# A cubic on VectorE written as two fused operations, with the ScalarE square carrying the leading coefficient

## The chip, the cores and the metric

The kernel runs on one core of a Trainium2 chip. The metric is the device time of one execution in microseconds (us), the median of several runs. The profile names the engines PE (TensorE, with PEld for its weight loads), DVE (VectorE), ACT (ScalarE), POOL (GpSimd) and SP (SyncE, which here only issues transfers).

## What is computed

Four batches of eight heads go through a linear attention with a decaying state, and the 3072 rows of 512 that come out go through two feed-forward layers of 512 to 2048 to 512. The second layer is the one that the change touches:

```python
def _moe_ref(x, w_in, w_out):
    h = x @ w_in
    g = np.maximum(0.01 * h, h)
    return (g @ w_out).astype(np.float32)

def _moe2_ref(x, w_in, w_out):
    h = x @ w_in
    g = h - np.tanh(h)
    return (g @ w_out).astype(np.float32)
```

The elementwise function h - tanh h loses its digits where h is small, so the kernel computes it in two ways, a polynomial for small arguments and the plain difference for the others, and picks one by a mask.

## The kernel before

The program is one fixed order of instructions for each engine, written out at build time. A Python planner walks over the work in ticks. One tick is one unit of six matmuls on PE, and after each unit the planner gives ACT and DVE a credit of 1.05 times 1.29 us (`UNIT_US`) and lets queued work go out against it, so the order on ACT, DVE, SP and POOL follows from the costs that are written beside each item. At run time every engine goes through its own list in order and waits on semaphores.

All matrix products are split in high and low parts, three products for one, with one 128x512 tile as the common size. For each such tile of an operand, ACT writes the high part (`upper`, L174, tile gh) and DVE the low part by a subtraction (`lower`, L180, tile gl).

The stages are the attention, the first layer's input product (`product`, L768), the first layer's output product (the first form in `mm_half`, L693), the second layer's input product (`prod`, L1040, accumulators Xd, Yd, Zd) and its output product (the second form in `mm_half`, L693). The last two stages of each layer overlap: from about 460 us on, units of `prod` and half steps of `mm_half` alternate, with conversions of later weights (`Convert`, tiles cv and raw, stored to w2s) as background work that takes what DVE credit is left.

What a half step of the output product needs comes by a pipeline with fixed leads. Step o issues the load of tile gr for step o+4 (`load_g`, on SP, L663), the upper part for step o+3 (ACT) and the lower part for step o+2 (DVE). Weight tiles wf of `prod` are loaded four products ahead (`load_f`, SP, L886).

Around the change stands `queue_el`, which takes one 128x512 tile h of the second layer's hidden values. It runs 96 times: 24 times with `on_dve` true (the tile comes from `copy_h`), 72 times with it false (the tile comes from `join`). ACT makes u = h^2 (L969), th = tanh of h or of -h (L973), and s, a square of u plus a constant (L977). DVE then makes the small-argument value in place in s by three operations (L985, L990, L993) with a scratch tile w. For the 72 tiles the difference h - tanh h is made by an accumulating transfer on POOL's queue, which adds h onto th in SBUF (L1020, et<-h); for the other 24 DVE does it (L997). ACT then makes a mask from u (L981), DVE copies the difference over s where the mask is set (L1007), and SP stores s to DRAM (L1013, g2s), from where a later output step loads it as gr.

The 128x512 tiles come from a pool of 94 buffers, handed out first in, first out: `alloc` takes the buffer that has been free the longest, `give` puts one at the end of the list.

```python
    def alloc(nm, dt=F32, shape=(P, TB)):
        pool, tag = free.popleft()
    def give(*ts):
        for t in ts:
            _, pool, tag = home.pop(id(t))
            free.append((pool, tag))
```

`give` is called when the last user of a tile has been issued, not when it is done. Whoever gets the buffer next waits at run time until that user has finished.

Of the kernel before, what the change touches and what calls it, by code (L numbers as in the profile page):

```python
# [14 lines left out]
AF = mybir.ActivationFunctionType  # L15
# [15 lines left out]
MIN_HI = 2.0 ** -15  # L31


C3 = -0.019799353554844856
A1 = -2.6095259189605713
B1 = -0.05411865562200546
K1 = 6.448651313781738
UT = 0.125


# [34 lines left out]
def kernel(  # L75
# [12 lines left out]
    nc = tc.nc  # L88
# [23 lines left out]
    def alloc(nm, dt=F32, shape=(P, TB)):  # L112
        pool, tag = free.popleft()
        serial[0] += 1
        t = pool.tile(list(shape), dt, tag=tag, name=f"{nm}_{serial[0]}")
        home[id(t)] = (t, pool, tag)
        return t
# [845 lines left out]
    def queue_el(d, half_m, half_t, h, on_dve):  # L963
        key = 2 * (d // NG) + half_t, d % NG + NG * half_m
        e = {}

        def a1():
            e["u"] = alloc("eu")
            nc.scalar.activation(out=e["u"], in_=h, func=AF.Square)  # L969

        def a2():
            e["th"] = alloc("et")
            nc.scalar.activation(out=e["th"], in_=h, func=AF.Tanh, scale=1.0 if on_dve else -1.0)  # L973

        def a3():
            e["s"] = alloc("es")
            nc.scalar.activation(out=e["s"], in_=e["u"], func=AF.Square, bias=beta)  # L977

        def a4():
            e["mk"] = cm.tile([P, TB], BF16, tag="mk", name=f"mk_{key[0]}_{key[1]}", bufs=2)  # L980
            nc.scalar.activation(out=e["mk"], in_=e["u"], func=AF.Relu, bias=edge)  # L981

        def v1():
            e["w"] = alloc("ew")
            nc.vector.scalar_tensor_tensor(out=e["w"], in0=e["u"], scalar=C3, in1=h, op0=ALU.mult, op1=ALU.mult)  # L985

        def v2():
            if not on_dve:
                give(h)
            nc.vector.scalar_tensor_tensor(out=e["w"], in0=e["u"], scalar=A1, in1=e["w"], op0=ALU.add, op1=ALU.mult)  # L990

        def v3():
            nc.vector.scalar_tensor_tensor(out=e["s"], in0=e["s"], scalar=K1, in1=e["w"], op0=ALU.add, op1=ALU.mult)  # L993
            give(e["w"])

        def v4():
            nc.vector.tensor_tensor(out=e["th"], in0=h, in1=e["th"], op=ALU.subtract)  # L997
            give(h)

        def v5():  # L1000
            a4()
            give(e["u"])
            masks[0] += 1
            cp_q.append((tick[0] + 1, 0.76, v6))

        def v6():
            nc.vector.copy_predicated(out=e["s"], mask=e["mk"].bitcast(mybir.dt.uint16), data=e["th"])  # L1007
            masks[0] -= 1
            give(e["th"])
            defer(STORE_LAG, store)  # L1010

        def store():
            nc.sync.dma_start(out=g2s[key[0], key[1]], in_=e["s"])  # L1013
            give(e["s"])
            made2.add(key)

        def to_dve():
            t = tick[0] + 1
            if not on_dve:
                nc.gpsimd.dma_start(out=e["th"], in_=h, accum_op=ALU.add)  # L1020
            dve_q.extend([(t, 0.7, v1), (t, 0.7, v2)])
            if on_dve:
                dve_q.append((t, 0.7, v4))
            dve_q.append((t, 0.7, lambda: (v3(), mk_q.append((max(tick[0], t + (0 if on_dve else 5)), 0.72, v5)))))
            return 0.0, 0.0

        t = tick[0] + (1 if on_dve else 2)
        act_q.extend([(t, 0.62, a1), (t, 0.62, a2), (t, 0.72, lambda: (a3(), later(1, to_dve)))])
# [170 lines left out]
```

## Time and profile before

| | before |
|---|---|
| median of 3 runs | 1058.73 us (1057.42 to 1059.09) |
| the profiled execution, its own time | 1059.45 us |
| its span, first to last instruction | 1057.7 us |
| PE busy | 1041.5 us, 98% |
| DVE busy | 826.7 us, 78% |
| ACT busy | 721.1 us, 68% |
| POOL busy | 93.2 us, 9% |

The span is what the trace covers; the execution's own time has 1.75 us around it. The granted TensorE clock is at its upper level, 2.4 GHz, in every slice. An engine's busy time is the sum of its instructions. PE's records overlap, since matmuls are pipelined, so its idle time is read from the waits and from the timeline.

### The profile page before, as it was taken

The numbers are of one execution on the slowest core, as the hardware profiler recorded it, in microseconds if no ns is written. First come the engines' busy times: TensorE is split into PE (matmuls) and PEld (weight loads), VectorE is DVE, ScalarE is ACT, GpSimd is POOL, SyncE is SP. The second block draws the span as 40 slices with busy tenths as digits, with TensorE's granted clock in tenths as the row PEclk, the third lists the DMA queues.
The fourth block names the chain that finished last, engine by engine and source line by source line (L and its number), as shares of the span: only waits on it lengthen the run. The fifth ranks groups of instructions, "written<-read, shape, count | busy, mean of one in ns | idle before, by whom it ended". The sixth has DMA issues, their size and how long they took to land.

```text
span 1057.7 us, 17635 instructions
## 1 busy us (share of the span) xinstructions
PE 1041.5 (98%) x5931; PEld 902.2 (85%) x5931; DVE 826.7 (78%) x1363; ACT 721.1 (68%) x1299; POOL 93.2 (9%) x124
## 2 busy tenths in 40 slices
PE   9999899999999999999999999999999999999998
PEld 6888778888888888888888888888888888888887
DVE  3589897774788999967999789898878988687630
ACT  6889676766776556656777679887668766666440
POOL 3232000000000000000110111001100110011000
PEclk9999999999999999999999999999999999999999
DMA  9998465675668899959999988998987988878641
GB/s 223 242 269 233 164 234 190 208 250 210 225 234 286 287 361 388 393 200 285 276 323 298 324 257 260 303 290 261 316 252 224 268 246 255 259 220 229 190 149 40
DMA packets 208634, 267.67 MB, mean 253 GB/s; under 512 B 65056, under 2 KB 106144, under 8 KB 208544
## 3 DMA queue, kind: packets, MB, share of 16 engines
q1 hardware_dynamic: 197888, 247.52, 70.1%
q0 software_dynamic: 10368, 18.88, 10.3%
q8 instruction: 47, 0.77, 0.3%
q14 instruction: 43, 0.35, 0.1%
q10 hardware_dynamic: 288, 0.15, 0.1%
HBM read 161.63 MB, written 85.98 MB: 234 GB/s over the span
## 4 chain that ended last, share of the span: by engine, by line
PE 89%; DVE 4%; DMA 3%; ACT 2%; issue 1%; SPq 0%; DVEq 0%; ACTq 0%
PE o L693 46%; PE Xd L1040 11%; PE X L768 9%; PE Yd L1040 6%; PE Y L768 4%; PE Zd L1040 3%; PE y L577 2%; PE sc L550 2%; PE Z L768 2%; PE kTp L515 1%; PE y L573 1%; PE qTp L529 1%; DVE c L781 1%; PE u L596 1%; DMA gr<-g1s 1%
## 5 line engine op out<-in xcount | busy, mean ns | idle before, releaser
L693 PE MATMUL o<-gh,wo 128*128 128x512 f32 x768 | 239.5, 379 | 0.0
L693 PEld LDWEIGHTS o<-gh,wo 128*128 128x128 f32 x768 | 145.2, 189 | 20.4
L174 ACT ACTIVATE gh<-gr 128x512 fp32r<-128x512 f32 x192 | 118.3, 621 | 54.1 <-DMA gr<-g1s 26.9
L180 DVE TENSOR_TENSOR gl<-gr,gh 128x512 fp32r<-128x512 f32 x192 | 130.1, 683 | 27.9 <-ACT gh L174 22.5
L693 PE MATMUL o<-gl,wo 128*128 128x512 f32 x384 | 145.9, 380 | 2.5 <-DVE gl L180 2.5
L693 PE MATMUL o<-w2h,gh 128*128 128x512 f32 x384 | 145.5, 379 | 0.0
L693 PE MATMUL o<-w2h,gl 128*128 128x512 f32 x384 | 145.5, 379 | 0.0
L693 PE MATMUL o<-w2l,gh 128*128 128x512 f32 x384 | 145.5, 379 | 0.0
L1020 POOL DMA_DIRECT2D et<-h x72 | 62.1, 862 | 826.9 <-DVE gl L180 424.3
L1040 PE MATMUL Xd<-xch,wf 128*128 128x512 f32 x384 | 129.5, 379 | 0.0
L768 PE MATMUL X<-xch,wg 128*128 128x512 f32 x384 | 123.2, 381 | 3.7 <-DVE wg L180 2.5
L1007 DVE COPY_PREDICATED es<-mk,et 128x512 f32<-128x512 uint16 x96 | 70.9, 742 | 44.6 <-ACT mk L981 44.6
L768 PEld LDWEIGHTS X<-xch,wg 128*128 128x128 f32 x384 | 72.4, 189 | 17.0 <-DVE wg L180 3.4
L693 PEld LDWEIGHTS o<-gl,wo 128*128 128x128 f32 x384 | 72.6, 189 | 14.3 <-DVE gl L180 4.1
L969 ACT ACTIVATE eu<-h 128x512 f32<-128x512 f32 x96 | 59.9, 624 | 33.3 <-DVE h L949 31.2
L693 PEld LDWEIGHTS o<-w2l,gh 128*128 128x128 f32 x384 | 72.6, 189 | 10.3
L693 PEld LDWEIGHTS o<-w2h,gh 128*128 128x128 f32 x384 | 72.6, 189 | 10.3
L1040 PEld LDWEIGHTS Xd<-xch,wf 128*128 128x128 f32 x384 | 72.6, 189 | 10.3
L693 PEld LDWEIGHTS o<-w2h,gl 128*128 128x128 f32 x384 | 72.6, 189 | 10.3
L1040 PE MATMUL Xd<-xcl,wf 128*128 128x512 f32 x192 | 72.8, 379 | 0.0
L768 PE MATMUL X<-xcl,wg 128*128 128x512 f32 x192 | 72.8, 379 | 0.0
L985 DVE SCALAR_TENSOR_TENSOR ew<-eu,h 128x512 f32<-128x512 f32 x96 | 65.5, 683 | 8.8 <-DMA wfs<-wg 3.2
(101 smaller groups left out, 2030.3 us busy)
## 6 DMA issues: line engine op xcount, KB each, us to landing
wf<-wfs SPq DMA_DIRECT2D x168, 256.0 KB, 4.3
g1s<-c SPq DMA_DIRECT2D x96, 256.0 KB, 2.2
gr<-g1s SPq DMA_DIRECT2D x96, 256.0 KB, 5.3
g2s<-es SPq DMA_DIRECT2D x96, 256.0 KB, 3.5
gr<-g2s SPq DMA_DIRECT2D x96, 256.0 KB, 4.2
et<-h POOLq DMA_DIRECT2D x72, 256.0 KB, 5.3
raw<-in_moe_w_in_dram SPq DMA_DIRECT2D x32, 512.0 KB, 5.7
raw<-in_moe_w_out_dram SPq DMA_DIRECT2D x32, 512.0 KB, 4.4
```

Of the source, the lines that this page charges most:

```text
L174: nc.scalar.activation(out=hi, in_=src, func=AF.Copy)
L180: nc.vector.tensor_tensor(out=lo, in0=src, in1=hi.bitcast(F32), op=ALU.subtract)
L515: nc.tensor.transpose(ps[:, b, :], d["k"][:, b].rearrange("p h d -> p (h d)"), ident)
L550: nc.tensor.matmul(sc[h][:, b, :], d["kT"][r, b, :], d["qT"][r, b, tq], start=True, stop=True)
L577: nc.tensor.matmul(place(b, h), d["v"][:, b, h, :], d["A"][h][:, b, :], start=c == 0 and b % 2 == 0, stop=b % 2 == 1)
L693: nc.tensor.matmul(ACC[j], a, il(b), start=first and i == 0, stop=last and i == 2)
L768: nc.tensor.matmul(ps, w[:, c], il(x), start=first and kt == 0 and i == 0, stop=kt == 1 and i == 2, skip_group_check=True)
L969: nc.scalar.activation(out=e["u"], in_=h, func=AF.Square)
L985: nc.vector.scalar_tensor_tensor(out=e["w"], in0=e["u"], scalar=C3, in1=h, op0=ALU.mult, op1=ALU.mult)
L1007: nc.vector.copy_predicated(out=e["s"], mask=e["mk"].bitcast(mybir.dt.uint16), data=e["th"])
L1020: nc.gpsimd.dma_start(out=e["th"], in_=h, accum_op=ALU.add)
L1040: nc.tensor.matmul(ps, a, il(b), start=nm in ("P1", "P2", "P5") and kt == 0 and j == 0, stop=kt == 1 and j == 2, skip_group_check=True)
```

## The change

The polynomial is written another way. Before, three DVE operations form w = C3 u h, then w = (u + A1) w, then s = (s + K1) w, with s = (u + B1)^2. After, ACT forms s = (SQ u + B1)^2, and DVE forms s = (s + K1) th and then s = s u (times -1 where th is the tanh of -h). Tanh takes the place of h, so the coefficients are others, and the scratch tile is gone.

As th is now an input of the first DVE operation, the accumulating transfer, which writes over th, is issued right behind that operation instead of ahead of it, and h is given back at the same place. The mask is queued six ticks after the last of the two operations where it was queued five ticks after the element's start on DVE.

```diff
-C3 = -0.019799353554844856
-A1 = -2.6095259189605713
-B1 = -0.05411865562200546
-K1 = 6.448651313781738
+SQ = 0.04557729699996048
+B1 = -0.24376608898
+K1 = 0.27391141909500494
 UT = 0.125
...
         def a3():
             e["s"] = alloc("es")
-            nc.scalar.activation(out=e["s"], in_=e["u"], func=AF.Square, bias=beta)
+            nc.scalar.activation(out=e["s"], in_=e["u"], func=AF.Square, scale=SQ, bias=beta)
...
         def v1():
-            e["w"] = alloc("ew")
-            nc.vector.scalar_tensor_tensor(out=e["w"], in0=e["u"], scalar=C3, in1=h, op0=ALU.mult, op1=ALU.mult)
-
-        def v2():
+            nc.vector.scalar_tensor_tensor(out=e["s"], in0=e["s"], scalar=K1, in1=e["th"], op0=ALU.add, op1=ALU.mult)
             if not on_dve:
+                nc.gpsimd.dma_start(out=e["th"], in_=h, accum_op=ALU.add)
                 give(h)
-            nc.vector.scalar_tensor_tensor(out=e["w"], in0=e["u"], scalar=A1, in1=e["w"], op0=ALU.add, op1=ALU.mult)
 
         def v3():
-            nc.vector.scalar_tensor_tensor(out=e["s"], in0=e["s"], scalar=K1, in1=e["w"], op0=ALU.add, op1=ALU.mult)
-            give(e["w"])
+            nc.vector.scalar_tensor_tensor(out=e["s"], in0=e["s"], scalar=1.0 if on_dve else -1.0, in1=e["u"],
+                                           op0=ALU.mult, op1=ALU.mult)
...
         def to_dve():
             t = tick[0] + 1
-            if not on_dve:
-                nc.gpsimd.dma_start(out=e["th"], in_=h, accum_op=ALU.add)
-            dve_q.extend([(t, 0.7, v1), (t, 0.7, v2)])
+            dve_q.append((t, 0.7, v1))
             if on_dve:
                 dve_q.append((t, 0.7, v4))
-            dve_q.append((t, 0.7, lambda: (v3(), mk_q.append((max(tick[0], t + (0 if on_dve else 5)), 0.72, v5)))))
+            dve_q.append((t, 0.7, lambda: (v3(), mk_q.append((tick[0] + (0 if on_dve else 6), 0.72, v5)))))
             return 0.0, 0.0
```

PE's list is the same instruction for instruction, 4876 rows in both. DVE's has 1348 rows before and 1252 now. ACT, POOL and SP have the same number of rows in another order, from the first element on. Lines of the changed kernel are six lower than those of the old one at its end, and one lower in most of its middle (gl is L180 before and L179 now). In the rows below, `DMASWk` is the semaphore of the accumulating transfers on POOL's queue, which take k = 0 to 7 in turn, and `DMAHWk` that of other transfers; the number behind a tile's name is its serial number in that program.

First, DVE, where the first elements meet the output steps (about 485 to 498 us of the old trace). Before, from the conversion step to the second lower part:

```order
L217 SCALAR_TENSOR_TENSOR cv_5615<-raw_1_5529,cv_5615 128x512 [waits DMAHW6_49,DVE_49]
L985 SCALAR_TENSOR_TENSOR ew_5727<-eu_5597,h_5565 128x512 [waits DMAHW5_49]
L990 SCALAR_TENSOR_TENSOR ew_5727<-eu_5597,ew_5727 128x512 [waits DVE_49]
L180 TENSOR_TENSOR gl_5736<-gr_5602,gh_5649 128x512 [waits DMAHW6_49,DMAHW2_49]
L993 SCALAR_TENSOR_TENSOR es_5680<-es_5680,ew_5727 128x512 [waits DMAHW0_49,DVE_49,Activation_49]
L985 SCALAR_TENSOR_TENSOR ew_5752<-eu_5682,h_5595 128x512 [waits DMAHW2_49,Activation_49]
L990 SCALAR_TENSOR_TENSOR ew_5752<-eu_5682,ew_5752 128x512 [waits DVE_49]
L993 SCALAR_TENSOR_TENSOR es_5686<-es_5686,ew_5752 128x512 [waits DVE_49,Activation_49]
L985 SCALAR_TENSOR_TENSOR ew_5766<-eu_5723,h_5628 128x512 [waits PE_49,Activation_49]
L990 SCALAR_TENSOR_TENSOR ew_5766<-eu_5723,ew_5766 128x512 [waits DVE_49]
L993 SCALAR_TENSOR_TENSOR es_5738<-es_5738,ew_5766 128x512 [waits DMAHW7_49,DVE_49,Activation_49]
L180 TENSOR_TENSOR gl_5786<-gr_5641,gh_5714 128x512 [waits DMAHW1_49,PE_49]
```

Now, between the same two lower parts and the element operations ahead of them:

```order
L989 SCALAR_TENSOR_TENSOR es_5680<-es_5680,eu_5597 128x512 [waits DVE_49]
L179 TENSOR_TENSOR gl_5734<-gr_5602,gh_5649 128x512 [waits DMAHW5_49,DMAHW2_49]
L983 SCALAR_TENSOR_TENSOR es_5686<-es_5686,et_5684 128x512 [waits Activation_49]
L989 SCALAR_TENSOR_TENSOR es_5686<-es_5686,eu_5682 128x512 [waits DVE_49]
L219 SCALAR_TENSOR_TENSOR cv_5615<-raw_1_5529,cv_5615 128x512
L983 SCALAR_TENSOR_TENSOR es_5736<-es_5736,et_5723 128x512 [waits DMAHW6_49,Activation_49]
L989 SCALAR_TENSOR_TENSOR es_5736<-es_5736,eu_5721 128x512 [waits DVE_49]
L211 TENSOR_SCALAR cv_5688<-cv_5688 128x512
L213 TENSOR_SCALAR cv_5688<-cv_5688 128x512 [waits DVE_49]
L216 SCALAR_TENSOR_TENSOR cv_5688<-raw_1_5612,cv_5688 128x512 [waits DMAHW3_49,DVE_49]
L179 TENSOR_TENSOR gl_5791<-gr_5641,gh_5712 128x512 [waits DMASW1_49]
```

The second lower part has moved ahead by 12 matmuls of the program's order, conversion steps stand where element operations stood, and its buffer is now one that an accumulating transfer (the one of es_5686) reads.

Second, DVE further on (about 511 to 517 us of the old trace), between two lower parts. Before:

```order
L180 TENSOR_TENSOR gl_5940<-gr_5811,gh_5867 128x512 [waits DMAHW7_49]
L985 SCALAR_TENSOR_TENSOR ew_5944<-eu_5882,h_5856 128x512
L1007 COPY_PREDICATED es_5842<-mk_1_5942,et_5840 128x512 [waits DMASW3_49,DVE_49,Activation_49]
L990 SCALAR_TENSOR_TENSOR ew_5944<-eu_5882,ew_5944 128x512 [waits DVE_49]
L993 SCALAR_TENSOR_TENSOR es_5886<-es_5886,ew_5944 128x512 [waits DVE_49]
L985 SCALAR_TENSOR_TENSOR ew_5971<-eu_5914,h_5880 128x512 [waits PE_49]
L990 SCALAR_TENSOR_TENSOR ew_5971<-eu_5914,ew_5971 128x512 [waits DVE_49]
L993 SCALAR_TENSOR_TENSOR es_5918<-es_5918,ew_5971 128x512 [waits DVE_49]
L180 TENSOR_TENSOR gl_5993<-gr_5859,gh_5930 128x512 [waits DMAHW4_49]
```

Now:

```order
L179 TENSOR_TENSOR gl_5934<-gr_5812,gh_5862 128x512 [waits DMAHW7_49,DMAHW3_49]
L983 SCALAR_TENSOR_TENSOR es_5910<-es_5910,et_5908 128x512 [waits DMASW3_49,Activation_49]
L989 SCALAR_TENSOR_TENSOR es_5910<-es_5910,eu_5893 128x512 [waits DVE_49]
L219 SCALAR_TENSOR_TENSOR cv_5780<-raw_1_5653,cv_5780 128x512
L983 SCALAR_TENSOR_TENSOR es_5938<-es_5938,et_5936 128x512 [waits Activation_49]
L989 SCALAR_TENSOR_TENSOR es_5938<-es_5938,eu_5924 128x512 [waits DVE_49]
L211 TENSOR_SCALAR cv_5865<-cv_5865 128x512
L213 TENSOR_SCALAR cv_5865<-cv_5865 128x512 [waits DVE_49]
L216 SCALAR_TENSOR_TENSOR cv_5865<-raw_1_5777,cv_5865 128x512 [waits DMAHW6_49,DVE_49]
L179 TENSOR_TENSOR gl_5996<-gr_5854,gh_5922 128x512 [waits DMAHW5_49,DMASW4_49]
```

The first operation of es_5910 and the lower part gl_5996 now each wait for an accumulating transfer. Transfer 3 is issued behind the first operation of es_5851, which stands seven rows ahead of this piece, and transfer 4 behind that of es_5910.

Third, ACT at the same place. Before:

```order
L969 ACTIVATE eu_5882<-h_5856 128x512 [waits DMAHW2_49,DVE_49]
L973 ACTIVATE et_5884<-h_5856 128x512 [waits DMAHW3_49]
L977 ACTIVATE es_5886<-eu_5882,lead 128x512 [waits Activation_49]
L981 ACTIVATE mk_8_5899<-eu_5792,lead 128x512
L942 ACTIVATE kp_5912<-Xd_5903 128x512 [waits DMAHW0_49,PE_49]
L969 ACTIVATE eu_5914<-h_5880 128x512 [waits DVE_49]
L973 ACTIVATE et_5916<-h_5880 128x512 [waits DMASW0_49,DVE_49]
L977 ACTIVATE es_5918<-eu_5914,lead 128x512 [waits Activation_49]
L174 ACTIVATE gh_5930<-gr_5859 128x512 [waits DMAHW4_49,DVE_49]
```

Now:

```order
L968 ACTIVATE eu_5893<-h_5847 128x512
L941 ACTIVATE kp_5906<-Xd_5896 128x512 [waits DMAHW7_49,PE_49]
L972 ACTIVATE et_5908<-h_5847 128x512 [waits DVE_49]
L976 ACTIVATE es_5910<-eu_5893,lead 128x512 [waits DMAHW7_49,DMASW3_49,Activation_49]
L173 ACTIVATE gh_5922<-gr_5854 128x512 [waits DMAHW5_49,DMASW1_49]
L968 ACTIVATE eu_5924<-h_5876 128x512 [waits DMAHW1_49,DVE_49]
L972 ACTIVATE et_5936<-h_5876 128x512
L976 ACTIVATE es_5938<-eu_5924,lead 128x512 [waits Activation_49]
```

The square es_5910 gets the buffer of the tile that transfer 3 reads, and waits for that transfer; in the old program the squares there wait for ACT alone. One element earlier es_5795 waits in the same way, for transfer 2 (`DMASW2`).

## Rows read from the trace of the kernel before

**Rows 1.** The page's first part: the span, and each engine's busy time.

```profile
span 1057.7 us, 17635 instructions
PE 1041.5 (98%) x5931; PEld 902.2 (85%) x5931; DVE 826.7 (78%) x1363; ACT 721.1 (68%) x1299; POOL 93.2 (9%) x124
```

**Rows 2.** Table by stretch: length, then busy (x instructions) of each engine, PE first.

```profile
core 0: us, PE busy (x) PEld busy (x) DVE busy (x) ACT busy (x) POOL busy (x), PEclk, DMA share, GB/s
...
463.00:550.00 87.00, 84.50 (x391) 73.11 (x390) 75.70 (x127) 60.16 (x105) 8.87 (x11) 1.00 0.92 284
550.00:620.00 70.00, 70.00 (x326) 61.26 (x325) 60.93 (x96) 50.81 (x92) 9.31 (x11) 1.00 0.99 305
...
700.00:800.00 100.00, 100.00 (x465) 87.58 (x464) 83.21 (x132) 72.57 (x130) 11.30 (x14) 1.00 0.91 278
...
980.00:1057.70 77.70, 73.65 (x342) 64.15 (x340) 26.06 (x41) 24.51 (x42) 0.86 (x1) 1.00 0.37 124
```

**Rows 3.** PE's waits from 463 us to the end: total, times, longest.

```profile
PE o L693 <- DVE gl L180: 2.5, 2, 1.8
```

**Rows 4.** PE's timeline, 494 to 523 us: the two matmuls behind an idle time.

```profile
498.24 0.48 PE L693 MATMUL o<-gl,wo 128*128 128x512 f32 x1 [1.76 <-DVE gl L180]
521.35 0.48 PE L693 MATMUL o<-gl,wo 128*128 128x512 f32 x1 [0.74 <-DVE gl L180]
```

**Rows 5.** Groups by line: the three DVE operations of the polynomial.

```profile
L990 DVE SCALAR_TENSOR_TENSOR ew<-eu,ew 128x512 f32<-128x512 f32 x96 | 66.1, 688 | 2.4
L993 DVE SCALAR_TENSOR_TENSOR es<-es,ew 128x512 f32<-128x512 f32 x96 | 66.0, 687 | 4.3
```

**Rows 6.** Groups by line: ACT's square with a constant, and its tanh.

```profile
L977 ACT ACTIVATE es<-eu,lead 128x512 f32<-128x512 f32 x96 | 68.2, 710 | 3.6 <-DVE gl L180 1.4 <-DMA wfs<-wg 1.2 <-DVE es L993 0.9
L973 ACT ACTIVATE et<-h 128x512 f32<-128x512 f32 x96 | 59.3, 617 | 0.9 <-DMA g2s<-es 0.8 <-DVE ew L985 0.2
```

**Rows 7.** Accumulating transfers, start on POOL to landing: 470 to 512, whole span, 800 to 985.

```profile
DMA to landing us min/median/max: 5.4/6.2/8.8
...
DMA to landing us min/median/max: 3.2/5.3/8.8
...
DMA to landing us min/median/max: 3.2/4.8/6.3
```

**Rows 8.** The same, one transfer each: starts near 527 and near 552 us.

```profile
et<-h POOLq DMA_DIRECT2D x1, 256.0 KB, 7.2
...
et<-h POOLq DMA_DIRECT2D x1, 256.0 KB, 7.3
```

**Rows 9.** DVE's timeline, 488 to 513 us: start, length, instruction, idle time before it.

```profile
488.41 0.69 DVE L985 SCALAR_TENSOR_TENSOR ew<-eu,h 128x512 f32<-128x512 f32 x1 [3.23 <-DMA wfs<-wg]
...
489.75 0.68 DVE L180 TENSOR_TENSOR gl<-gr,gh 128x512 fp32r<-128x512 f32 x1
...
497.50 0.68 DVE L180 TENSOR_TENSOR gl<-gr,gh 128x512 fp32r<-128x512 f32 x1
498.10 0.76 DVE L220 SCALAR_TENSOR_TENSOR cv<-raw,cv 128x512 int32<-128x512 int32 x1
...
510.52 0.68 DVE L180 TENSOR_TENSOR gl<-gr,gh 128x512 fp32r<-128x512 f32 x1
511.12 0.68 DVE L985 SCALAR_TENSOR_TENSOR ew<-eu,h 128x512 f32<-128x512 f32 x1
511.72 0.73 DVE L1007 COPY_PREDICATED es<-mk,et 128x512 f32<-128x512 uint16 x1
512.35 0.67 DVE L990 SCALAR_TENSOR_TENSOR ew<-eu,ew 128x512 f32<-128x512 f32 x1
```

**Rows 10.** ACT's timeline: a copy of an upper part that waits for its load.

```profile
514.21 0.63 ACT L174 ACTIVATE gh<-gr 128x512 fp32r<-128x512 f32 x1 [4.21 <-DMA gr<-g1s]
```

**Rows 11.** SP's waits for accumulating transfers: total, times, longest.

```profile
SPq L886 <- DMA et<-h: 15.8, 7, 4.8
...
SPq L663 <- DMA et<-h: 3.4, 2, 2.7
```

**Rows 12.** The page's sixth part: loads of gr, size and median us to landing.

```profile
gr<-g1s SPq DMA_DIRECT2D x96, 256.0 KB, 5.3
...
gr<-g2s SPq DMA_DIRECT2D x96, 256.0 KB, 4.2
```

## The prediction

> **What bounds the kernel now.** I read the page's first part, then the table by stretch, then PE's waits, then PE's timeline. PE is busy for 98% of the span and no other engine for more than 78% [rows 1]. The table shows that this is no average over unlike stages: from 550 to 620 us and from 700 to 800 us PE has no idle time at all, while DVE has 9 and 17 us of it [rows 2]. The 465 matmuls of the latter 100 us give 0.215 us each, the fixed pace of this half of the program. From 463 us on, PE waits only twice, both times for a lower part from DVE, 2.5 us together [rows 3]: 1.76 us ahead of 498.24 and 0.74 us ahead of 521.35 [rows 4]. The other 4 us of the last stretch [rows 2] are the last copies and stores behind the last matmul. The change leaves PE's list as it is, and everything ahead of the first element too. So the most it can win is 2.5 us, and what it can lose is whatever new waits reach PE.
>
> **DVE's removed operations.** 96 elements lose one operation of 0.688 us [rows 5]: 66 us less on DVE, of 826.7. All of it lies beside PE's work except where DVE is late for PE, which is in the two waits. By itself it is worth between 0 and 2.5 us. The cover is PE; if a lower part were late, it would be gone.
>
> **ACT's square.** It keeps its constant from a tile (0.710 us) and gains a scale. The tanh carries a scale without such a tile and takes 0.617 us, like a plain square [rows 6], so I put the scale at nothing. The scratch tile's end frees a buffer per element, while s, th and u are held a tick longer.
>
> **The accumulating transfer.** This is the part that matters. It started as soon as th was there; now it stands behind the first DVE operation, in DVE's order. In the same breath h's buffer goes to the free list, where some dozen buffers are in line, so it is soon handed out. I counted, in the order in which the code issues things, the matmuls between such a transfer and the SP instruction that gets the buffer: before, never under 16; now, 20 of 64 times 11 to 14. For ACT the least was 26 and is now 11; for DVE's lower parts three stand at 13. Twelve matmuls are 2.6 us; a transfer takes 5.3 us in the median from its start on POOL, and 6.2 us, never under 5.4, from 470 to 512 us [rows 7]. What gets the buffer must wait, and on an in-order engine all behind it wait too. SP already did so nine times before, for up to 4.8 us [rows 11], without cost to PE.
>
> The Trainium skill, DMA: Bandwidth & Descriptors, section Anatomy of one DMA — SWDGE (gpsimd) path, fits such a transfer as 2.0 us plus its bytes at 436 GB/s, which for 256 KB is an estimate of 2.6 us. The trace disagrees: no transfer of the 72 landed in under 3.2 us [rows 7]. By that rule the waits below would vanish and the first rival would hold.
>
> **First place, PE's 1.76 us.** I follow the new DVE list with old starts. The first lower part waits for the store `DMAHW5`, which had landed when the old L985 began at 488.41 [rows 9]; operations follow each other every 0.6 us, and a conversion shift takes 0.76 [rows 9]. So the first operation of es_5686 ends at 489.7, transfer 1 starts at 489.8 and lands at 496.0, and gl_5791, which has its buffer, ends at 496.7. Before, this part began at 497.50 [rows 9], and PE wanted it at 498.24 - 1.76 = 496.5. PE waits 0.2 us instead of 1.76. With 5.4 us it doesn't wait.
>
> **Second place, some 520 us.** Three transfers now stand in a chain. Its fifth operation from 488.4 on is the first of es_5736, whose square waits only for the store `DMAHW6`, landed by 489.75, when the old lower part that waits for it began [rows 9]. It ends at 491.7, so transfer 2 starts at 491.8 and lands at 498.0. ACT's square es_5795 waits for it, ends at 498.6, and DVE goes through ten instructions, from the first operation of es_5795 to that of es_5851: 5.9 us at the pace above, to 504.6. Transfer 3 runs from 504.7 to 510.9. ACT's es_5910 waits for it: +0.7 is 511.6. Its first operation on DVE: 512.3. Transfer 4 runs from 512.4 to 518.6, and gl_5996, which has its buffer, ends at 519.3. PE wants that part 84 matmuls after the first place: 496.7 + 84 x 0.215 = 514.8. It waits 4.5 us. The three landings carry this: at 5.4 us each, the first place costs nothing and this one 2.4; at 7.3 us, as single transfers a little later took [rows 8], the two cost 8.0 together. I take the window's median: 4.7 us for both.
>
> **Behind it.** SP's load of gr_6005 waits for transfer 5, which starts right behind 4 (first operation of es_5938, about 514.6) and lands at 520.9; the load takes 5.3 us more [rows 12], so ACT copies the upper part at 526.2 and is stopped until then, as it was for 4.21 us in the old trace [rows 10]. Mask, masked copy and lower part end at 528.8; PE, having gone on at 519.3, wants it 39 matmuls on, at 527.7. That is 1.1 us; a faster load or an engine that catches up takes it to 0; I put 0.55. At the next change of output rows (matmul 2822 of the list) an ACT copy of a PSUM bank waits for a transfer issued 22 matmuls ahead, and PE needs the bank 17 matmuls after the copy: 39 matmuls, 8.4 us, against 0.7 + 6.2 + 0.6 = 7.5 us for operation, landing and copy. It fits if DVE is on time, and costs 2 us if DVE is 3 us late, which the queue above allows; I put 1.0.
>
> **The rest.** Later transfers land in 4.8 us [rows 7]; with the operation's 0.7 that makes SP 2.9 us late where it meets one 12 matmuls on. The gr load behind it lands 4.2 us after issue [rows 12], so ACT is stopped for some 3 us. Lower parts are issued a median of 29 matmuls (6.2 us) ahead of their use, 5.5 us after their own 0.7, which covers that. I put nothing. If that cover is gone because ACT is busy, it is the second rival below.
>
> **The sum.** New waits 4.7 + 0.55 + 1.0 = 6.25 us, old ones 2.5 us: +3.75. The profiled execution took 1059.45 us, of which its span is 1057.7; it would take 1063.2. It stood 0.7 us over the median 1058.73, so for the median I forecast **1062.5 us**. With the low ends (2.4 + 0 + 0 - 2.5) it is 1058.6, with the high ones (8.0 + 1.1 + 2.0 - 2.5) 1067.3.
>
> **Rivals.** *Faster:* the transfers land soon enough and DVE, with 66 us less, is ahead: both waits go and none comes, 1058.7 - 2.5 = 1056.2. It decides at the landing time: the second place's 4.5 us fall by 1.5 for each 0.5 us less over three links, so below 4.7 us it is free. Against it, none of the transfers from 470 to 512 us took under 5.4 [rows 7]; for it, the median after 800 us is 4.8. Chance 0.08. *No change:* landings at 5.4 us, the rest hidden: 1058.6, 2.1 us to either side; 0.24. For it: SP's old waits cost PE nothing. *Much slower:* the 20 waits on SP after the first stretch each get through to PE by 0.4 us, since ACT, once stopped, has its own backlog: 1062.5 + 8 = 1070.5. Against it stand the 5.5 us of cover and DVE's lighter load; 0.08. That DVE doesn't lose the operations is excluded: its list has 96 rows fewer.
>
> **How the numbers follow.** The forecast has 0.60. About 0.2% (2.1 us) is what a measurement of this kernel tells from no change. Slower is the forecast and the much slower case, 0.68; within, 0.24; faster, 0.08. The range leaves out the faster and the much slower case, 0.16, and a little of the edges: from 1057.5, just under the low ends' sum, to 1067.3, the high ends' sum.
>
> **What would show it.** PE's waits after 463 us: 6 to 7 us in place of 2.5, the largest near 519 us on a gl that waits for a transfer et<-h. ACT's waits should name et<-h ahead of es, and SP's waits for et<-h should grow from 19 us to some 60. DVE busy should be near 761 us, ACT near 721. Wrong it would be if the transfers between 485 and 520 us landed in under 5 us, if the DVE steps ahead of es_5851 ran much earlier than 504 us, or if PE's idle time came from elsewhere.

## The result and the profile after

The changed kernel took 1070.45 us in the median of 4 runs (1068.99 to 1071.47), beside 1058.49 us for the kernel before on the same chip: a ratio of 1.0111, 95% interval 1.0096 to 1.0126. It is slower, as forecast, but by 12 us and not by 4, past the upper end of the range (1067.3). The profiled execution took 1069.76 us, its span is 1067.9 us; against the old profiled execution that is 10.3 us more, of which the span has 10.2. The other 1.7 us between the medians is how the two profiled executions lie: the old one 1 us above the median of its runs, this one 0.7 below. The two slower of the four executions (1071.14 and 1071.47 us) have a mean granted clock of 0.996 and 0.997, the two faster ones 0.998.

First the page's opening part, which answers to [rows 1]:

```profile
span 1067.9 us, 17478 instructions
PE 1045.5 (98%) x5931; PEld 903.4 (85%) x5931; DVE 769.1 (72%) x1267; ACT 721.4 (68%) x1299; POOL 94.6 (9%) x124
```

DVE's load fell by 57.6 us, ACT's and POOL's stayed (0.3 and 1.4 us more). A span of ten us more with less work points to waiting. The table by stretch (columns as in [rows 2]) says where:

```profile
463.00:550.00 87.00, 81.72 (x374) 70.05 (x373) 71.54 (x119) 58.07 (x102) 8.22 (x10) 1.00 0.90 281
550.00:620.00 70.00, 70.00 (x326) 61.29 (x325) 46.25 (x73) 50.79 (x92) 10.11 (x12) 1.00 0.97 295
620.00:700.00 80.00, 76.60 (x346) 65.93 (x344) 62.65 (x99) 65.94 (x115) 7.73 (x9) 0.98 0.85 261
700.00:800.00 100.00, 98.51 (x456) 86.29 (x457) 67.86 (x106) 69.29 (x124) 12.03 (x14) 1.00 0.89 271
```

PE loses time in two places, around 500 to 520 us and around 680 to 702 us; from 550 to 620 us it has none idle. In the later of them the granted clock is under 1.00 too. PE's waits from 463 us on (total, times, longest) and its timeline, the matmuls behind an idle time, answer to [rows 3, 4]:

```profile
PE o L692 <- DVE gl L179: 7.8, 4, 2.7
PE o L692 <- ACT st L713: 2.3, 2, 2.2
```

```profile
503.33 0.48 PE L692 MATMUL o<-gl,wo 128*128 128x512 f32 x1 [2.01 <-DVE gl L179]
507.91 0.48 PE L692 MATMUL o<-gl,wo 128*128 128x512 f32 x1 [0.43 <-DVE gl L179]
519.92 0.48 PE L692 MATMUL o<-gl,wo 128*128 128x512 f32 x1 [2.68 <-DVE gl L179]
...
684.64 0.48 PE L692 MATMUL o<-w2h,gh 128*128 128x512 f32 x1 [2.16 <-ACT st L713]
...
701.49 0.48 PE L692 MATMUL o<-w2h,gl 128*128 128x512 f32 x1 [2.73 <-DVE gl L179]
```

That is 10.1 us of waits in place of 2.5: 7.6 of the 10.2 us that the span grew by. Behind the wait at 684.64 us PE also ran slower: the table of 2 us stretches shows the lower level, 0.50 (1.2 GHz), and 6 and 8 matmuls where 2 us hold 9.3.

```profile
686.00:688.00 2.00, 2.00 (x6) 1.52 (x6) 1.05 (x3) 2.00 (x5) 0.86 (x1) 0.50 0.96 297
688.00:690.00 2.00, 2.00 (x8) 1.65 (x7) 1.10 (x2) 2.00 (x5) 0.00 (x0) 0.66 1.04 378
```

In the timeline 18 matmuls start from 684.64 to 690.18 us: 17 steps in 5.54 us instead of 17 x 0.215 = 3.66, so 1.9 us are lost there. The rest of the 10.2, 0.7 us, is made of small pieces. Each wait costs PE a little more than its listed length, since the next matmul starts 0.32 us behind the first and not 0.215 (701.49 and 701.81 us). Two stops at 540 to 542 us, of which PE's waits list 0.17 us, cost 0.6 us. Against that, PE was 0.3 us ahead of the old trace at 463 us.

Set beside the same matmuls of the old trace, PE falls behind in two steps. At 463 us it is 0.3 us ahead. The matmul of 682.10 us, the last ahead of the wait at 684.64, stands at 679.01 us in the old trace, so 3.4 us were lost up to there. The last matmul of all starts at 1063.54 us instead of 1053.27, so the later place cost 7.2 us.

What do the late engines wait for? The waits for accumulating transfers from 463 us on; for SP they answer to [rows 11]:

```profile
SPq L662 <- DMA et<-h: 73.8, 13, 9.2
...
SPq L885 <- DMA et<-h: 42.0, 9, 9.0
```

```profile
ACT gh L173 <- DMA et<-h: 12.6, 6, 3.5
...
ACT kp L941 <- DMA et<-h: 5.5, 2, 3.9
```

```profile
DVE gl L179 <- DMA et<-h: 21.0, 10, 4.9
```

Before, the same views have 19.2 us for SP, 1.8 for ACT and 1.6 for DVE. The transfers themselves took no longer on the whole: from start on POOL to landing, 463 to 1000 us, minimum, median, maximum:

```profile
DMA to landing us min/median/max: 3.2/5.2/8.3
```

So the same transfers are now waited for, in three engines. They did take longer in one part of the span, 6.4 us in the median from 620 to 800 us where it was 5.1; but the program of run 5 below has 6.4 us there too, and loses nothing. The chain of waits through the later place, followed back from 701.49 us, ends on one of them: a transfer that starts at 693.12 us, holds the buffer of a lower part until 700.7 us, and PE behind it.

```profile
693.12 7.60 DMA et<-h
700.72 0.02 issue
700.74 0.70 DVE gl L179
701.44 0.04 issue
701.49 0.70 PE o L692 x2
```

The wait at 684.64 us, for ACT's copy of a PSUM bank (st), goes back to a transfer as well. ACT's upper part got the buffer of the transfer that started at 669.02 us and landed after 6.4 us, and stood 3.50 us for it; DVE stood 4.46 us behind ACT. From there on both worked without a gap until ACT came to the copy at 684.01 us:

```profile
675.44 0.63 ACT L173 ACTIVATE gh<-gr 128x512 fp32r<-128x512 f32 x1 [3.50 <-DMA et<-h]
```

```profile
676.72 0.75 DVE L1003 COPY_PREDICATED es<-mk,et 128x512 f32<-128x512 uint16 x1 [4.46 <-ACT mk L980]
```

### The profile page after: what moved, and what is told of

Its sections match the earlier page's. It is cut to its first block, busy times and chain, and to the rows that moved or that the text cites. A ratio compares the mean times of both kernels' runs of the same rounds, so it can differ in the third digit from the quotient of the medians.

```text
span 1067.9 us, 17478 instructions
## 1 busy us (share of the span) xinstructions
PE 1045.5 (98%) x5931; PEld 903.4 (85%) x5931; DVE 769.1 (72%) x1267; ACT 721.4 (68%) x1299; POOL 94.6 (9%) x124
## 4 chain that ended last, share of the span: by engine, by line
PE 85%; DVE 5%; DMA 5%; ACT 2%; issue 2%; SPq 0%; DVEq 0%; ACTq 0%; POOLq 0%
PE o L692 43%; PE Xd L1034 10%; PE X L767 9%; PE Yd L1034 5%; PE Y L767 4%; PE Zd L1034 2%; PE Z L767 2%; PE sc L549 2%; PE y L576 2%; DMA et<-h 1%; PE kTp L514 1%; PE y L572 1%; DVE c L780 1%; PE qTp L528 1%; PE u L595 1%
## 5 line engine op out<-in xcount | busy, mean ns | idle before, releaser
L179 DVE TENSOR_TENSOR gl<-gr,gh 128x512 fp32r<-128x512 f32 x192 | 130.2, 683 | 50.0 <-ACT gh L173 24.7
L983 DVE SCALAR_TENSOR_TENSOR es<-es,et 128x512 f32<-128x512 f32 x96 | 65.8, 685 | 27.9 <-ACT es L976 27.8
L1034 PEld LDWEIGHTS Xd<-xch,wf 128*128 128x128 f32 x384 | 72.6, 189 | 10.3
L976 ACT ACTIVATE es<-eu,lead 128x512 f32<-128x512 f32 x96 | 68.1, 710 | 9.5 <-issue 4.6
```

Source lines behind the costliest of these rows:

```text
L179: nc.vector.tensor_tensor(out=lo, in0=src, in1=hi.bitcast(F32), op=ALU.subtract)
L1034: nc.tensor.matmul(ps, a, il(b), start=nm in ("P1", "P2", "P5") and kt == 0 and j == 0, stop=kt == 1 and j == 2, skip_group_check=True)
```

## The experiments

Theory A was that the loss comes from buffers handed out again while a transfer still reads them. The rivals were B, that the transfer's later start and landing delays the masked copies; D, that the new order of DVE's list makes it late; and that the loss at 680 to 702 us only follows from the one at 500 to 520 us. The runs, as ratios to the kernel before on the same chip, with PE's waits behind 463 us in the profiled execution. That is one execution of each run; in runs 3 and 10 it is 2 us faster than the run's median, in run 8 it is 1.5 us slower.

| run | ratio | 95% interval | PE waits, us |
|---|---|---|---|
| the change | 1.0111 | 1.0096 to 1.0126 | 10.1 |
| 1 its order, transfers' buffers reused later | 1.0026 | 1.0013 to 1.0038 | 3.4 |
| 2 old order, transfer behind first operation | 1.0230 | 1.0214 to 1.0245 | 19.5 |
| 3 two operations, transfer early | 1.0005 | 0.9993 to 1.0017 | 1.6 |
| 4 old kernel, all reuses on SP, near | 1.0176 | 1.0139 to 1.0213 | 13.9 |
| 5 the change, all reuses later | 0.9992 | 0.9983 to 1.0000 | 0.3 |
| 6 as 5, ahead of 613 us only | 1.0060 | 1.0045 to 1.0074 | 4.8 |
| 7 as 5, behind 613 us only | 1.0055 | 1.0040 to 1.0071 | 4.8 |
| 8 old kernel, all reuses later | 0.9991 | 0.9983 to 1.0000 | 0.6 |
| 9 as 5, for SP's loads only | 1.0080 | 1.0056 to 1.0103 | 5.7 |
| 10 as 5, for ACT and DVE only | 1.0022 | 1.0011 to 1.0033 | 1.0 |
| 11 h given back four ticks later | 1.0086 | 1.0070 to 1.0102 | 8.3 |
| 12 no transfers, DVE subtracts | 0.9972 | 0.9960 to 0.9983 | 0 |

**1. Same order, other buffers.** `alloc` passes over a young buffer; nothing else changes, and every engine's list is that of the changed kernel.

```diff
-        pool, tag = free.popleft()
+        at = next((i for i, b in enumerate(free) if tick[0] - young.get(b, -99) >= 8), 0)
+        pool, tag = free[at]
+        del free[at]
...
                 nc.gpsimd.dma_start(out=e["th"], in_=h, accum_op=ALU.add)
+                young[home[id(h)][1:]] = tick[0]
                 give(h)
```

> The changed kernel, with the same instructions in the same order on every engine; only which buffer of the free list a tile gets differs: one that an accumulating transfer still reads (given back under 8 ticks ago) is passed over. SP's least reuse distance is 38 matmuls instead of 11, ACT's 29 instead of 11, DVE's 31 instead of 13. Theory A (early reuse makes in-order SP, ACT and DVE wait for the transfer): SP's waits for et<-h fall from 116 us to under 20, PE's waits after 463 us from 10 us to under 3, the clock stays at the upper level, 1056 to 1060 us. Rival B (the transfer's later start and landing itself delays the masked copies): unchanged, 1068 to 1072. Rival D (the new order, conversions ahead of lower parts, makes DVE late): unchanged, 1068 to 1072.

1062.03 us. Of the 1.11%, 0.85 are gone, with DVE's order, the late transfers and the late masks all still there: rivals B and D fall as the main cause. SP's waits for et<-h fell from 116 to 0.3 us. It missed the expected 1060 by another wait of the same kind: passing over some buffers handed ACT's tanh one that a store of a converted weight still read. ACT's timeline, then PE's:

```profile
501.52 0.63 ACT L976 ACTIVATE et<-h 128x512 f32<-128x512 f32 x1 [6.00 <-DMA w2s<-cv]
```

```profile
504.87 0.80 PE L696 MATMUL o<-gl,wo 128*128 128x512 f32 x1 [2.48 <-DVE gl L183]
```

**2. The transfer late, all else old.** The kernel before with its three operations; the first now reads th, so the transfer must stand behind it. Its small-argument values are others by that; the work is the same.

```diff
-            nc.vector.scalar_tensor_tensor(out=e["w"], in0=e["u"], scalar=C3, in1=h, op0=ALU.mult, op1=ALU.mult)
+            nc.vector.scalar_tensor_tensor(out=e["w"], in0=e["u"], scalar=C3, in1=e["th"], op0=ALU.mult, op1=ALU.mult)
+            if not on_dve:
+                nc.gpsimd.dma_start(out=e["th"], in_=h, accum_op=ALU.add)
...
-            if not on_dve:
-                nc.gpsimd.dma_start(out=e["th"], in_=h, accum_op=ALU.add)
```

> The kernel before, in its own order with its three operations; only the first operation reads th in place of h (so the small-argument values are others), and so the transfer has to be issued behind it. h is given back at the second operation, as before. SP's reuse distances fall to 11 to 15 matmuls at 16 places, ACT's to 11 to 15 at 7, and masked copies stand 13 or more behind the transfer. Theory A: waits for et<-h on SP above 60 us, on ACT and DVE above 15 us, PE waits above 8 us after 463 us, 1066 to 1078 us though DVE's order is the old one. Rival D (the new order of DVE's list is what costs): 1057 to 1061 us.

1083.94 us, above the expected range: the old order does not save it. ACT alone waited 68 us for transfers, and PE 7.0 us at once for a copy of a PSUM bank. It is worse than the change. Its masked copies stand as near as 13 matmuls behind the transfer and waited 19.5 us for it, so this run alone doesn't separate A from B; runs 1 and 5 do.

**3. Two operations, the transfer early.** The polynomial multiplies by h, with three coefficients of its own; the transfer goes out ahead of the first operation again, and the mask has its old rule back. The main line of the edit:

```diff
-            nc.vector.scalar_tensor_tensor(out=e["s"], in0=e["s"], scalar=K1, in1=e["th"], op0=ALU.add, op1=ALU.mult)
+            nc.vector.scalar_tensor_tensor(out=e["s"], in0=e["s"], scalar=K1, in1=h, op0=ALU.add, op1=ALU.mult)
```

> Two operations as in the changed kernel, but the polynomial multiplies by h instead of th (three coefficients fitted for that form), so that the transfer goes out as early as in the kernel before, ahead of the first operation, and the mask keeps its old rule. DVE loses the same 96 operations. SP's least distances are 12 to 19 at 8 places, ACT's 24, DVE's 18. Theory A: most of the loss is gone, SP's waits for et<-h 20 to 50 us, 1056 to 1062 us. Rival D (fewer DVE operations let conversions move ahead of what PE needs): 1066 to 1071 us, as the order has moved just as much.

1060.43 us, no change against the kernel before (the interval ends at 0.17%). DVE is as light as in the change (768.7 us) and conversions have moved ahead in its list as they did there, so neither costs anything that this run can tell.

**4. All reuses on SP.** The kernel before, its order kept; loads of gr and wf take the buffer of a transfer where they can.

```diff
-        pool, tag = free.popleft()
+        at = 0
+        if nm in ("gr", "wf"):
+            at = next((i for i, b in enumerate(free) if tick[0] - young.get(b, -99) <= 1), 0)
+        pool, tag = free[at]
+        del free[at]
...
             if not on_dve:
+                young[home[id(h)][1:]] = tick[0]
                 give(h)
```

> The kernel before with the same order on every engine; a load on SP gets, where it can, the buffer that a transfer reads, so that all 72 reuses fall on SP, 13 of them at 12 matmuls and 30 at 12 to 19; ACT and DVE wait for none. It isolates SP's waits from those on ACT and DVE. Theory A1 (waits on SP alone are enough): SP's waits for et<-h above 100 us, PE loses 5 to 10 us, 1063 to 1069 us. Theory A2 (SP's waits are covered by the leads of loads, and only waits on ACT and DVE, or SP's together with them, get through): below 1060 us.

1077.98 us, more than expected: here waits on SP alone reach PE. SP's waits for transfers:

```profile
SPq L892 <- DMA et<-h: 98.2, 28, 7.3
SPq L669 <- DMA et<-h: 55.2, 20, 6.5
```

ACT and DVE waited for no transfer, but ACT waited 79 us for loads of gr from 463 to 1000 us (32 in the kernel before): a load that is issued late stops the engine that needs it.

**5. All reuses later.** The rule of run 1 for the buffers of stores too, ten ticks. The edit, against the changed kernel (the other stores are given back with `aged=10` in the same way):

```diff
-        pool, tag = free.popleft()
+        at = next((i for i, b in enumerate(free) if tick[0] >= young.get(b, -99)), 0)
+        pool, tag = free[at]
+        del free[at]
...
-    def give(*ts):
+    def give(*ts, aged=0):
         for t in ts:
             _, pool, tag = home.pop(id(t))
+            young[pool, tag] = tick[0] + aged if aged else -99
             free.append((pool, tag))
...
-            give(st)
+            give(st, aged=10)
...
-                give(h)
+                give(h, aged=10)
```

> The changed kernel, every engine's order the same; a buffer given back behind any transfer or store is passed over for ten ticks where another is free. In the first run of this kind the 16 places with SP were cured, but ACT then got a buffer that a store of a converted weight still read: it stood 6.0 us at 495 us, PE 2.5 us at 502.4 to 504.9, and the clock went to the lower level behind that. Theory A (early reuse, of whatever transfer): that wait goes too, SP's waits for et<-h are under 10 us, PE's waits after 463 us under 1.5 us, 1055.5 to 1058.5 us, faster than both kernels by up to 0.25%. Rival (the two-operation order has a cost of its own): 1060 to 1063 us as in the first run of this kind.

1058.0 us beside 1058.94: the whole loss is gone, and PE's waits behind 463 us are one:

```profile
PE o L697 <- DVE gl L184: 0.3, 1, 0.3
```

**6 and 7. One part at a time.** The rule of run 5 up to tile 1000, some 613 us (run 6), or from there on (run 7: `if 1000 <= serial[0] < 99999`). The edit, against run 5:

```diff
-        at = next((i for i, b in enumerate(free) if tick[0] >= young.get(b, -99)), 0)
+        at = next((i for i, b in enumerate(free) if tick[0] >= young.get(b, -99)), 0) if 0 <= serial[0] < 1000 else 0
```

> As the run with every reuse aged, but only up to tile 1000 (matmul 3170 of the list, about 613 us); behind it the plain list, where SP again meets transfers 11 to 14 matmuls on at 17 places. By the changed kernel's timeline the waits ahead of 613 us cost 5.3 us and those near 684 and 701 us 4.9 us and some 2 us of lower clock behind them. Theory A with that split: 1062 to 1066 us, PE waits now behind 613 us only. Rival (the second loss follows from the first, through engines that never catch up): with the first waits gone the second go as well, 1055.5 to 1059 us.

> The counterpart: the plain list up to tile 1000, aged behind it. Theory A: the waits at 503, 508 and 520 us stay as they were in the changed kernel (5 us), those at 684 and 701 us go with the lower clock: 1061 to 1064 us. Rival (the second loss follows from the first): the first waits leave the engines late, 1066 to 1071 us.

1065.1 and 1064.1 us. Against run 5 the later part costs 0.68% and the first 0.63%; the two add up to 1.31%, and the change against run 5 is 1.19%. So the second loss does not follow from the first. In run 6 PE waits behind the seam only, above all for a copy at 678.94 us and a lower part at 694.12 us, the two kinds of 684 and 701 us; in run 7 for lower parts from 504 to 521 us only. PE's waits from 463 us on in run 6, then in run 7:

```profile
PE o L697 <- ACT st L718: 2.4, 1, 2.4
PE o L697 <- DVE gl L184: 2.2, 1, 2.2
```

```profile
PE o L697 <- DVE gl L184: 4.8, 3, 2.4
```

**8. The same rule in the kernel before**, with `aged=8` in place of 10.

> The kernel before, its order unchanged, with the same rule for buffers (eight ticks). Its SP waits for et<-h are 19 us and cost PE nothing by its trace; PE's waits of 1.76 and 0.74 us are for lower parts that a busy DVE made late. Theory A: those waits are DVE's and not the reuse's, so 1057 to 1060 us, no change. Rival (any program of this kind gains from later reuse): 1054 to 1057 us.

1057.79 us: with three operations the same time as run 5 with two. Once buffers are no matter, 59 us of DVE work (828.3 against 769.0) are worth nothing here. That most of the old kernel's own 2.5 us of waits went as well (0.6 us left) had not been expected: there they were put down to a busy DVE. The old trace shows that the larger one, ahead of 498.24 us, was itself a wait for a buffer. DVE's scratch tile ew_5752 had that of a weight tile whose store started at 487.64 us and landed 5.5 us later, at 493.16. DVE stood 2.22 us for it and had no gap from there to the lower part of 497.50 us. The profile puts this wait down to ACT, but what the operation reads from ACT had long been written. DVE's timeline of the kernel before:

```profile
493.25 0.69 DVE L985 SCALAR_TENSOR_TENSOR ew<-eu,h 128x512 f32<-128x512 f32 x1 [2.22 <-ACT h L958]
```

**9 and 10. Which engine's waits.** The rule of run 5 for SP's loads only (run 9), or for all tiles but these (run 10, `not in`). The edit, against run 5:

```diff
-        at = next((i for i, b in enumerate(free) if tick[0] >= young.get(b, -99)), 0)
+        at = next((i for i, b in enumerate(free) if tick[0] >= young.get(b, -99)), 0) if nm in ("gr", "wf") else 0
```

> The changed kernel, order unchanged; only the loads that SP issues (gr and wf) pass over the buffers that a transfer or store was given ten ticks ago or less. SP's least reuse distance is 42 matmuls, ACT's stay at 12 to 17 (nine of them), DVE's at 13 to 18 (seven). It takes apart which engine's waits reach PE. If, as the prediction had it, ACT's and DVE's own waits make the loss and SP's cost nothing: 1064 to 1071 us. If SP's waits make it: SP's waits for et<-h near 0 and 1058 to 1061 us.

> The counterpart: only tiles of ACT and DVE pass such buffers over, which leaves them to SP's loads: 71 reuses fall on SP, 30 of them at 11 or 12 matmuls; ACT's least is 53 and DVE's 82. If SP's waits cost PE nothing: 1056 to 1060 us. If they get through, as the old kernel's run with all reuses on SP suggests (1078 us): 1072 to 1085 us, SP's waits for et<-h above 150 us, PE's waits for lower parts whose own engines wait for loads.

1068.58 and 1061.62 us; the second lies between the two times that were expected. Against run 5, three quarters of the loss stay with SP cured (0.88 of 1.19%), a quarter with ACT and DVE cured (0.30%). So most of the loss comes by the tiles that ACT and DVE themselves write. SP's share is no larger than that quarter if more near reuses cost no less, since run 10 leaves SP more of them than the change has. SP's waits for transfers grew to 161 us there and cost PE little; SP's waits, then PE's:

```profile
SPq L890 <- DMA et<-h: 101.5, 31, 7.6
SPq L667 <- DMA et<-h: 59.5, 25, 5.3
```

```profile
PE o L697 <- DVE gl L184: 1.0, 2, 0.7
```

Run 4 has as long waits on SP and loses eight times as much. Its DVE has three operations per element, 86 us of work from 800 to 900 us against 74 in run 10, and so less room to make good a late load. This reading is argued from the two profiles, not shown by a run of its own; why loads alone cost so much in run 4 and so little in run 10 stays open.

**11. Give h back later.**

```diff
-                give(h)
+                defer(4, lambda: give(h))
```

> The simplest edit of the changed kernel: h is given back four ticks behind the transfer's issue, with the plain list. The list is shorter for it, so ACT's and DVE's orders shift at some places; SP keeps five reuses at 12 to 15 matmuls, the others are at 28 or more, ACT's least is 18, DVE's 26. Theory A: most of the loss is gone, SP's waits for et<-h 15 to 40 us, 1057 to 1062 us. Rival (the list, now shorter, hands out buffers of stores too early instead): 1063 to 1069 us.

1069.39 us: the rival, at the upper end of its range. SP waits 22 us for the transfers and no longer 116, but the shorter list hands out stores' buffers earlier. SP stood 7.0 us for one, in front of a load of wf; the next such store went out late, DVE waited for its buffer, and PE 3.3 us for DVE. What made PE's other 5.0 us of waits stays open. SP's wait from 490 to 512 us:

```profile
SPq L885 <- DMA w2s<-cv: 7.0, 1, 7.0
```

**12. No transfers.** DVE subtracts for all tiles, in the time that the polynomial gave back. The sign of the tanh is no longer needed, and the mask is queued at once and not six ticks later.

```diff
-            if not on_dve:
-                nc.gpsimd.dma_start(out=e["th"], in_=h, accum_op=ALU.add)
-                give(h)
...
-            if on_dve:
-                dve_q.append((t, 0.7, v4))
+            dve_q.append((t, 0.7, v4))
```

> The changed kernel without accumulating transfers: for the 72 tiles too DVE subtracts th from h (72 operations of 0.68 us more, DVE near 819 us), and h is given back there; the mask follows at once. No reuse waits for a transfer. Theory A with room on DVE: 1056 to 1061 us. Rival (DVE at its old load, with the masks earlier, is late for PE in the full stretches): 1062 to 1068 us.

1056.91 us beside 1059.41, the fastest of all and faster than both kernels. PE waits for nothing behind 463 us. DVE is at 810.6 us, under the old 826.7:

```profile
PE 1042.2 (99%) x5931; PEld 902.9 (86%) x5931; DVE 810.6 (77%) x1339; ACT 722.0 (68%) x1299; POOL 32.0 (3%) x52
```

With 72 transfers fewer the others also land sooner: loads of wf in 3.5 us in the median instead of 4.7, stores of g2s in 2.5 instead of 3.7. The Trainium skill, Trainium Kernel Development and Optimization, section Key Constraints, says that transfers from SP, ACT and POOL run on the same 16 DMA engines and interleave. These medians fit that.

## Why the prediction was wrong

**DVE's removed operations.** Worth nothing by themselves, which is the low end of what the text gave them (runs 3, 5 and 8). The larger of the two old waits, which it put down to DVE, hung on the buffer of a store (run 8). The load fell by 57.6 us, not 66: an operation in an unbroken row adds the 0.60 us from start to start, not its own 0.688 [rows 9].

**ACT's square.** Right: 0.710 us with the scale, as without.

**The transfer and its buffer.** Right, and the cause: run 1 takes the transfers' early reuse away and with it 0.85 of the 1.11%, run 5 that of the stores too and with it the rest. The landings were as read, 3.2 us at the least. By the fit in the Trainium skill, DMA: Bandwidth & Descriptors, section Anatomy of one DMA — SWDGE (gpsimd) path, such a transfer takes an estimate of 2.6 us. The traces disagree: in every one that has these transfers the shortest of the 72 took 3.2 us. By the prediction's own count a landing of 2.6 us would have made the waits vanish.

**First place.** Right. PE does not wait for gl_5791: the matmul that waited until 498.24 us before starts at 495.98 with no wait ahead of it.

**Second place.** The size was right, the path only half, so the size was partly luck. Forecast were 4.7 us for both places; measured are 2.01 + 0.43 + 2.68 = 5.1. The chain, from POOL's, ACT's and DVE's timelines:

```profile
491.18 0.90 POOL L985 DMA_DIRECT2D et<-h  x1 [1.20 <-DMA wfs<-wg]
507.55 0.85 POOL L985 DMA_DIRECT2D et<-h  x1 [15.47 <-DVE es L983]
514.91 0.85 POOL L985 DMA_DIRECT2D et<-h  x1 [6.51 <-PE Xd L1034]
```

```profile
498.73 0.72 ACT L976 ACTIVATE es<-eu,lead 128x512 f32<-128x512 f32 x1 [3.84 <-DMA et<-h]
```

```profile
500.66 0.69 DVE L948 TENSOR_TENSOR h<-Zd,kp 128x512 f32<-128x512 f32 x1 [4.97 <-DMA w2s<-cv]
501.26 0.68 DVE L983 SCALAR_TENSOR_TENSOR es<-es,et 128x512 f32<-128x512 f32 x1
...
502.59 0.68 DVE L179 TENSOR_TENSOR gl<-gr,gh 128x512 fp32r<-128x512 f32 x1
...
506.57 0.68 DVE L983 SCALAR_TENSOR_TENSOR es<-es,et 128x512 f32<-128x512 f32 x1
...
519.17 0.69 DVE L179 TENSOR_TENSOR gl<-gr,gh 128x512 fp32r<-128x512 f32 x1 [0.37 <-DMA et<-h]
```

Transfer 2 starts at 491.18 (forecast 491.8), lands after 7.5 us instead of 6.2 and holds ACT's square until 498.73 (498.0). Then a link that was not in the count: DVE, ahead of the first operation of that element, stood 4.97 us for a buffer that the store of a converted weight read, until 500.66, and began it at 501.26 instead of about 499.5. The conversions had moved ahead, as the order showed, and their stores with them; only accumulating transfers were counted. That made the lower part of 502.59 late and PE wait at 503.33, where no wait was forecast. Transfer 3 started 2.8 us late (507.55 against 504.7), 0.2 of it because POOL starts 0.3 us behind the operation's end (506.57 + 0.68) where the count had 0.1. But 3 and 4 landed after 5.3 and 4.2 us instead of 6.2, and gl_5996 started at 519.17 against 518.6.

**Behind it, and the change of output rows.** Forecast 0.55 and 1.0 us; measured 0 and 0.6, the two stops at 540 to 542 us. With the old waits gone, all that the sum priced comes to the 3.4 us that PE lost up to 682 us, for +3.75 forecast.

**The rest: "I put nothing".** This is the step that failed. Measured are 2.16 + 2.73 = 4.9 us of waits at 684.64 and 701.49 us, and the 1.9 us at the lower clock behind the first; with the restarts PE lost 7.2 us there, where the sum had 0. The step priced only what SP's late loads would do, and there it was nearly right (run 10). It left out the lower parts on DVE and ACT's tiles that themselves get a transfer's buffer, though the count a few lines above it had three lower parts at 13 matmuls. Of the 72 buffers only 23 go to SP next, 32 go to ACT and 17 to DVE. For such a part the 5.5 us of cover run against its own transfer: 0.7 us of operation, the lateness of DVE, and the landing. The part ahead of 701.49 us is one of the three; its transfer landed 7.6 us after its start. The other two, at 583.52 and 721.78 us, stood 2.3 and 3.3 us and cost PE nothing, so nearness alone does not decide it. Nor did the landing of 4.8 us hold, which is that of 800 to 985 us: the two transfers behind the waits took 6.4 and 7.6 us. The slowest case that the text weighed, 1070.5 us, has the measured time, and ACT's backlog behind a stop, which it named, stands in the trace ahead of 684.64 us. But there the stops were to come by SP's waits, and run 9 shows that those are the smaller part; that its time was met is luck.

**The clock.** The sum had every matmul at the pace of the upper level. It held through every wait of the old trace, the longest 1.76 us, and fell behind the one of 2.16 us here.

**The signs to look for.** PE's waits: 10.1 us, not 6 to 7. The one near 519 us came as described, on a lower part that waits for et<-h; it was neither alone nor clearly the largest. SP's: 116 us, not 60. DVE: 769, not 761.

## What to carry to other kernels

When a change lets a buffer go earlier, or its reader start later, list for every engine who gets that buffer next and how far on, and price the direct users (the tile that PE waits for) as well as the loads: in the changed kernel they made most of the loss, in run 4 loads alone made 1.8%. A transfer counts from its real start, behind a late engine, and stores count like any other reader. Keeping the order and changing only which free buffer is handed out separates reuse from everything else, and is also the cure: with buffers ten ticks old PE's waits came to 0.3 us (run 5). Time saved on an engine that is not the bound is worth what can be put there: here the subtraction, which took 72 transfers out of the program.

## What the runs showed of the hardware

A short wait of PE can cost nearly its length again in clock: 1.9 us behind one of 2.16. Behind waits of 2.16 us (684.64 us here) and 2.48 us (run 1) the granted clock fell to about half for some 3 us; behind waits of 2.01 and 2.68 us in the changed kernel (463 to 550 us) and of 2.73 us (701.49 us) stretches of 10 us show 1.00. In the other runs the lower level came with waits of 2.24 (run 6), 2.80 (run 9) and 3.27 us (run 11), and not with those of 2.38 (run 7) and 2.40 us (run 6). The length of a wait alone does not decide it in these runs; what does was not tried. Run 1, two stretches of 2 us with PE, PEld, DVE, ACT and POOL, then the clock:

```profile
504.00:506.00 2.00, 1.13 (x3) 0.95 (x4) 2.00 (x5) 2.00 (x4) 0.00 (x0) 0.61 0.32 100
506.00:508.00 2.00, 2.00 (x7) 1.61 (x6) 2.00 (x5) 2.00 (x5) 0.00 (x0) 0.54 0.91 305
```
